# A channel gate streamed through SBUF: three slots of 84 rows in place of four of 60, with smaller first tiles and gates in two parts

## The chip, the cores and the metric

The kernel runs on one core of one Trainium2 chip. The metric is device time in microseconds, the median of several runs. A run has one launch, with its inputs and its output in HBM. Beside the times there is one profiled execution, whose trace all views below are read from; its span runs from the first to the last instruction.

## The reference

The input `x` has 384 x 384 pixels of 384 channels in bf16, `w1d` is a single number. Each channel is averaged over all pixels, the average is multiplied by `w1d` and put through a sigmoid, and every pixel of the channel is multiplied by the result:

```python
g = jnp.einsum("bhwc->bc", x) / (H * W)
gp = jnp.pad(g, ((0, 0), (pad, pad)))          # k = 1, pad = 0
s = jnp.zeros_like(g)
for i in range(k):
    s = s + gp[:, i:i + C] * w1d[i]
s = _sigmoid(s)
return x * s[:, None, None, :]
```

The input and the output have 113.25 MB each. Taken literally, the input has to be read twice, since the mean needs all of it before the first product.

## The kernel before

**Tiling.** The pixels are spread over 128 partitions. One "row" in what follows is one pixel of 384 channels on each partition (768 B per partition), so there are 1,152 rows. A large SBUF buffer, `arena`, holds four slots of `TILE` = 60 rows and, behind them at `base`, the `FIRST` = 12 rows. The rest of the input makes 19 tiles of 60 rows, and tile k lives in slot k mod 4.

**The early gate.** The kernel guesses the gate: it sums only the first `EARLY` = 4 rows (`sum_first`, three matmuls with a matrix of ones), makes the sigmoid of that (`s_early`), and multiplies every tile by it as the tile comes in (`gate`, L204 to 207, a multiplication in place on VectorE). Meanwhile it also sums all of `x`: TensorE adds the first 52 rows of each tile (`sum_others`, 39 matmuls per tile into three PSUM banks), and VectorE the last `OWN` = 8 (`sum_own`, a reduction, L327, and an addition, L334). At the end the two sums are joined (`join_own`, `add_banks`), the true gate `s_true` is made (L474) and compared with `s_early` (L482 to 496). The flag `redo` says whether they differ in bf16. Only then would a second pass read everything again (`again`); it isn't run on these inputs.

**Order.** A small planner class (`Planner`) writes one list of instructions per engine in program order. For each instruction it derives the waits from the rows that it reads and writes. SP issues all loads but three halves, ACT issues all stores; an engine's list is strictly in order, so a wait holds up all that is behind it. Loads of the first four tiles are issued at once, three of them as two halves of 30 rows on SP and on ACT (`BOTH` = 3). One DMA of each queue is put ahead of the barrier at the kernel's start (`ahead`). From tile 4 on, a load waits for the store that empties its slot.

**The pause.** Ahead of the first such load stands `pause` (L387): a dummy activation on ACT that starts when store 0 has landed. ACT's list there is store 0, store 1, the pause, store 2.

**TensorE's loop.** The sums of the tiles are one hardware loop; each turn waits for one count of the semaphore `ready`, which GpSimd raises when a tile has landed (`relay`). Ahead of the loop TensorE waits for all `FIRST` rows (`plan.need`, L446). VectorE's gate of a tile has to wait for TensorE's sum of the same tile, because it overwrites the rows.

**The end.** The last tile is gated into another slot, so that its gate needn't wait for its sum. Then come its own reduction, the gate and the store of the 12 first rows, and the check. SP, ACT and VectorE read the flag, and ACT waits for all stores.

Of the kernel before, what the change touches and what calls it, by code (L numbers as in the profile page):

```python
# [3 lines left out]
P = 128  # L4
ROW = 384
BF16 = mybir.dt.bfloat16
# [3 lines left out]
ACT_F = mybir.ActivationFunctionType  # L10
# [139 lines left out]
def split(n, most):  # L150
    k = -(-n // most)
    return [n // k + (i < n % k) for i in range(k)]


WIDE = 512

FIRST, EARLY, TILE, SLOTS, BOTH, OWN, PAUSE = 12, 4, 60, 4, 3, 8, 8  # L160


def bass_standalone__channel_attn_eca__vision_kernel(
# [5 lines left out]
    B, H, W, C = x.shape  # L169
    assert B == 1 and C == ROW and (B * H * W) % (4 * P) == 0  # L170
    n_rows = B * H * W // P
    x_rows, o_rows = x.flatten_outer_dims(), out.flatten_outer_dims()

    def dram(view, r0, n):
        return view[r0 * P : (r0 + n) * P, :].rearrange("(p t) c -> p (t c)", p=P)

    ones = nc.alloc_sbuf_tensor("ones", [P, P], BF16)
    s_early = nc.alloc_sbuf_tensor("s_early", [P, C], BF16)
    w_one = nc.alloc_sbuf_tensor("w_one", [1, 16], BF16)
    w_scaled = nc.alloc_sbuf_tensor("w_scaled", [P, 2], F32)  # L180
    warm = nc.alloc_sbuf_tensor("warm", [P, 2], F32)
    wrong = nc.alloc_sbuf_tensor("wrong", [P, 1], F32)
    redo = nc.alloc_sbuf_tensor("redo", [P, 1], I32)
    total = nc.alloc_sbuf_tensor("total", [P, C], F32)
    own = nc.alloc_sbuf_tensor("own", [P, C], F32)
    part = nc.alloc_sbuf_tensor("part", [P, C], F32)
    terms = nc.alloc_sbuf_tensor("terms", [P, 3 * C], BF16)
    n_arena = nc.sbuf_bytes_remaining // (2 * C)
# [8 lines left out]
    def at(r0, n):  # L197
        assert r0 + n <= n_arena
        return arena[:, r0 * C : (r0 + n) * C]

    def rows(r0, n):
        return [("sb", r) for r in range(r0, r0 + n)]

    def gate(to, place, n, s):  # L204
        s_b = s[:].unsqueeze(1).broadcast_to([P, n, C])
        v, to_v = (at(r, n).rearrange("p (t c) -> p t c", t=n) for r in (place, to))
        return lambda e: e.tensor_tensor(to_v, v, s_b, ALU.mult)  # L207

    n_tiles = (n_rows - FIRST) // TILE
    base = SLOTS * TILE  # L210
    assert (n_rows - FIRST) % TILE == 0 and base + FIRST + 1 + PAUSE <= n_arena
    assert FIRST % 4 == EARLY % 4 == (TILE - OWN) % 4 == 0 and EARLY + 4 < FIRST
    last = n_tiles - 1
    ready = nc.alloc_semaphore("ready")

    def slot(k):
        return k % SLOTS * TILE

    def row0(k):
        return FIRST + k * TILE  # L220


    s_true = at(base + FIRST, 1)
    plan = Planner(nc, "a", 70)

    def load(place, n, r0, queues=("sync",), reads=()):
        i = 0
        for queue, m in zip(queues, split(n, -(-n // len(queues)))):
            plan.dma(
                queue,  # L230
                at(place + i, m),
                dram(x_rows, r0, n)[:, i * C : (i + m) * C],
                reads=reads,
                writes=rows(place + i, m),
            )
            i += m
# [19 lines left out]
    def add_rows(e, group, column, n, start, stop):  # L256

        n_wide = n * C // WIDE
        all_of = [
            mm(  # L260
                e,
                acc[group][i % 3][:, :],
                ones[:],
                arena[:, column + i * WIDE : column + (i + 1) * WIDE],
                start and i < 3,
                stop and i >= n_wide - 3,
            )
            for i in range(n_wide)
        ]
        return all_of[-1]  # L270
# [8 lines left out]

    def sum_others():  # L280

        def one(e, s):
            e.wait_ge(ready, 1).then_inc(ready, -1)  # L283
            add_rows(e, 1, slot(s) * C, TILE - OWN, False, False).then_inc(
                plan.sems["tensor"], 1
            )

        def emit(e):
            add_rows(e, 1, (base + EARLY) * C, 4, True, False)
            rounds = -(-n_tiles // SLOTS)  # L290
            some = n_tiles - (rounds - 1) * SLOTS
            with e.Fori(0, rounds) as k:
                for s in range(some):
                    one(e, s)
                if some < SLOTS:
                    with e.If(k < rounds - 1):
                        for s in range(some, SLOTS):
                            one(e, s)
            add_rows(
                e, 1, (base + EARLY + 4) * C, FIRST - EARLY - 4, False, True  # L300
            ).then_inc(plan.sems["tensor"], 1)

        plan.streams["tensor"].append(("block", emit, None))

# [15 lines left out]
    def sum_own(k):  # L320

        r0 = slot(k) + TILE - OWN
        view = at(r0, OWN).rearrange("p (t c) -> p c t", t=OWN)
        to = part if k else own
        plan.op(
            "vector",
            lambda e: e.reduce_sum(to[:], view, axis=mybir.AxisListType.X),  # L327
            reads=rows(r0, OWN),
            writes=["part" if k else "own"],
        )  # L330
        if k:
            plan.op(
                "vector",
                lambda e: e.tensor_tensor(own[:], own[:], part[:], ALU.add),  # L334
                reads=["own", "part"],
                writes=["own"],
            )
# [34 lines left out]
            writes=["total"],  # L372
        )

    def put(place, n, r0, to=None):
        to = place if to is None else to
        plan.op(
            "vector",
            gate(to, place, n, s_early),
            reads=["s_early"] + rows(place, n),  # L380
            writes=rows(to, n),
        )
        plan.final.append(
            plan.dma("scalar", dram(o_rows, r0, n), at(to, n), reads=rows(to, n))
        )

    def pause(r0):  # L387

        to = at(base + FIRST + 1, PAUSE)
        plan.op(  # L390
            "scalar",
            lambda e: e.activation(  # L392
                to, warm[:, 0:1].broadcast_to([P, PAUSE * C]), ACT_F.Sigmoid
            ),
            reads=["warm"],
            writes=rows(r0, 1) + ["pause"],
        )

    def weight():

# [23 lines left out]

    plan.op("gpsimd", lambda e: e.memset(warm[:, 0:1], 0.0), writes=["warm"])
    plan.op("vector", lambda e: e.memset(ones[:], 1.0), writes=["ones"])  # L426
    load(base, FIRST, 0)
    for k in range(BOTH):
        load(slot(k), TILE, row0(k), ("sync", "scalar"))
        if k == 0:  # L430
            plan.dma("scalar", w_one[0:1, 0:1], w1d.unsqueeze(0), writes=["w_one"])
    for k in range(BOTH, SLOTS):
        load(slot(k), TILE, row0(k))
    heads = {e: len(plan.streams[e]) for e in ("sync", "scalar")}
    weight()
    sum_first()
# [6 lines left out]
        reads=["total", "w_scaled0", "warm1"],  # L443
        writes=["s_early"],
    )
    plan.need("tensor", rows(base, FIRST))  # L446
    sum_others()

    for k in range(n_tiles):
        if k >= SLOTS:  # L450

            for i in range(2) if k == SLOTS else () if k < SLOTS + 2 else (k - SLOTS,):
                sum_own(i)
                put(slot(i), TILE, row0(i))
            if k == SLOTS:
                pause(slot(k))
            load(slot(k), TILE, row0(k), reads=["pause"] if k == SLOTS else ())
        there = rows(slot(k), TILE)
        plan.relay(ready, "gpsimd", "tensor", there, there, ["acc1"])
    plan.signals("tensor", rows(base, FIRST), ["acc1"])  # L460
    for k in range(n_tiles - SLOTS, last):
        sum_own(k)
        put(slot(k), TILE, row0(k))

    put(slot(last), TILE, row0(last), slot(n_tiles))
    sum_own(last)
    put(base, FIRST, 0)
    join_own()


# [30 lines left out]


    again = Planner(nc, "b", 30)
    half, r0 = base // 2, 0
    for k, n in enumerate(split(n_rows, half)):
        place = k % 2 * half
        again.dma("sync", at(place, n), dram(x_rows, r0, n), writes=rows(place, n))
        again.op(
            "vector",
            gate(place, place, n, s_true),  # L510
            reads=rows(place, n),
            writes=rows(place, n),
        )
        again.final.append(
            again.dma("scalar", dram(o_rows, r0, n), at(place, n), reads=rows(place, n))
        )
        r0 += n
# [4 lines left out]
    def ahead(name, e, n):  # L522

        block = nc.main_func.blocks[0].instructions
        at_end = len(block)
        plan.emit(name, e, n)
        new = block[at_end:]  # L530
        del block[at_end:]
        barrier = next(
            i
            for i, ins in enumerate(block)
            if ins.engine == e.engine and isinstance(ins, mybir.InstDrain)
        )
        block[barrier:barrier] = new

    ahead("sync", nc.sync, 1)
    ahead("scalar", nc.scalar, 1)  # L540
    plan.emit("sync", nc.sync, heads["sync"] - 1)
    plan.emit("scalar", nc.scalar, heads["scalar"] - 1)

    with nc.Block() as block:
# [66 lines left out]
```

## Time and profile before

| | us |
|---|---|
| median of 3 runs (lowest, highest) | 528.31 (528.24, 528.57) |
| the profiled execution | 528.49 |
| its span | 527.0 |
| TensorE matmuls busy | 198.5 |
| VectorE busy | 353.9 |
| ScalarE busy | 5.5 |
| mean DMA rate over the span | 430 GB/s |
| a store of 60 rows (5,760 KB), issue to landing, median | 47.4 |
| a load of 60 rows, issue to landing, median | 38.9 |

In the page's view of slices, each of the 40 columns is 13.2 us; the row "DMA" gives the busy share of the 16 DMA engines in tenths and the row below it what they moved. A line of the timeline reads: start, duration, engine, source line, operation, what is written and read, shape, and in brackets how long the engine stood idle before it and what ended that. A line with "SPq" or "ACTq" is the issue of a DMA by that engine's queue, not the transfer; where several are merged, the duration runs from the first to the last. In the view of waits the columns are the total, the number of waits and the longest.

### The profile page before, as it was taken

The page shows a single profiled execution, that of the slowest core. Times are in us where ns is not written, and L with a number is a line of the kernel's source. Part 1 is how long each engine was busy: PE and PEld are TensorE (multiplying, and loading weights), DVE is VectorE, ACT ScalarE, POOL GpSimd, SP SyncE. Part 2 cuts the span into 40 slices and gives each one's busy share as a digit, 9 for nine tenths or more (in the row PEclk, how much of TensorE's full clock was granted, in tenths as well). Part 3 has the DMA queues.
Part 4 walks back from the last instruction along what each step waited for, and adds up shares of the span by engine and source line. Part 5 has one row for each costly group of instructions (what it writes and reads, how often), then busy time and mean ns, then how long its engine had stood idle before and what let it go on. Part 6 is the DMA issues. An engine that isn't in the chain of part 4 may idle for free. (4 is left out here: it accounts for less than half of the span.)

```text
span 527.0 us, 1015 instructions
## 1 busy us (share of the span) xinstructions
PE 198.5 (38%) x754; PEld 0.2 (0%) x2; DVE 353.9 (67%) x81; ACT 5.5 (1%) x5; POOL 0.3 (0%) x5
## 2 busy tenths in 40 slices
PE   0389170070706151524333342516060707070810
PEld 0000000000000000000000000000000000000000
DVE  0639999649494858576666666666666666758892
ACT  1000020000000000000000000000000000000000
POOL 0000000000000000000000000000000000000000
PEclk9999766576767667675758585858585858585765
DMA  9999999999999999999999999999999999999998
GB/s 383 434 421 418 448 448 395 444 448 448 395 444 448 448 395 444 448 444 399 444 448 444 399 444 448 445 399 444 444 444 406 441 444 444 406 441 444 444 406 363
DMA packets 6196, 226.51 MB, mean 430 GB/s; under 512 B 690, under 2 KB 690, under 8 KB 690
## 3 DMA queue, kind: packets, MB, share of 16 engines
q10 hardware_dynamic: 3314, 122.10, 53.6%
q1 hardware_dynamic: 2880, 104.40, 46.1%
q14 instruction: 2, 0.02, 0.0%
HBM read 113.25 MB, written 113.25 MB: 430 GB/s over the span
## 5 line engine op out<-in xcount | busy, mean ns | idle before, releaser
L244 PE MATMUL acc<-arena,ones 128*128 128x512 bf16 x749 | 196.6, 429 | 288.4 <-PEq L283 288.4
L207 DVE TENSOR_TENSOR arena<-arena,s_early 128x23040 bf16<-128x23040 bf16 (+1 forms) x20 | 233.5, 11677 | 78.0 <-PE acc L244 73.6
L327 DVE TENSOR_REDUCE part<-arena 128x384 f32<-128x3072 bf16 x18 | 96.4, 5355 | 67.3 <-DMA arena<-in_x_dram 67.3
L334 DVE TENSOR_TENSOR own<-own,part 128x384 f32<-128x384 f32 x18 | 10.0, 558 | 0.6
L418 DVE TENSOR_SCALAR w_scaled<-w_all 128x1 f32<-128x1 f32 x2 | 0.2, 152 | 14.3 <-PE w_all L409 14.3
L409 PE MATMUL w_all<-w_one,ones 1*128 1x1 bf16 x1 | 0.2, 158 | 15.3 <-DMA w_one<-in_w1d_dram 15.3
L244 PE MATMUL acc_own<-terms,ones 128*128 128x384 bf16 x3 | 1.4, 479 | 10.5 <-DVE terms L345 10.5
L327 DVE TENSOR_REDUCE own<-arena 128x384 f32<-128x3072 bf16 x1 | 5.3, 5305 | 0.0
L474 ACT ACTIVATE arena<-total,w_scaled 128x384 bf16<-128x384 f32 x1 | 0.6, 615 | 439.0 <-DVE total L315 439.0
L315 DVE TENSOR_TENSOR total<-total,acc 128x128 f32<-128x128 f32 (+2 forms) x11 | 4.5, 408 | 0.4
L392 ACT ACTIVATE arena<-warm 128x3072 bf16<-128x3072 f32 x1 | 2.8, 2763 | 54.1 <-DMA out_dram<-arena 54.1
L313 DVE COPY total<-acc 128x384 f32<-128x384 f32 x1 | 0.6, 558 | 1.2 <-PE acc L244 1.2
L403 ACT ACT_TABLE_LOAD x1 | 1.3, 1283 | 2.3 <-issue 2.3
L352 DVE TENSOR_TENSOR own<-own,terms 128x384 f32<-128x384 f32 x2 | 1.1, 558 | 0.1
L345 DVE CAST terms<-own 128x384 bf16<-128x384 f32 x3 | 1.1, 357 | 0.1
L482 DVE TENSOR_TENSOR total<-arena,s_early 128x384 f32<-128x384 uint16 x1 | 0.6, 557 | 0.7 <-ACT arena L474 0.7
L370 DVE TENSOR_TENSOR total<-total,acc_own 128x384 f32<-128x384 f32 x1 | 0.6, 554 | 0.6 <-PE acc_own L244 0.6
L426 DVE MEMSET ones<- 128x128 bf16 x1 | 0.2, 165 | 1.0 <-PEq L596 1.0
L440 ACT ACTIVATE s_early<-total,w_scaled 128x384 bf16<-128x384 f32 x1 | 0.6, 615 | 15.8 <-DVE total L315 15.8
L242 PE MATMUL acc<-arena,ones 128*128 128x512 bf16 x1 | 0.6, 608 | 0.0
L490 DVE TENSOR_REDUCE wrong<-total 128x1 f32<-128x384 f32 x1 | 0.6, 552 | 0.0
L403 ACT ACTIVATE warm<-warm 128x1 f32<-128x1 f32 x1 | 0.2, 203 | 0.0
(8 smaller groups left out, 0.9 us busy)
## 6 DMA issues: line engine op xcount, KB each, us to landing
out_dram<-arena ACTq DMA_DIRECT2D x19, 5760.0 KB, 47.4
arena<-in_x_dram SPq DMA_DIRECT2D x16, 5760.0 KB, 38.9
arena<-in_x_dram ACTq DMA_DIRECT2D x3, 2880.0 KB, 27.4
arena<-in_x_dram SPq DMA_DIRECT2D x3, 2880.0 KB, 36.4
arena<-in_x_dram SPq DMA_DIRECT2D x1, 1152.0 KB, 10.3
out_dram<-arena ACTq DMA_DIRECT2D x1, 1152.0 KB, 16.9
w_one<-in_w1d_dram ACTq DMA_DIRECT2D x1, 0.0 KB
```

What stands on the lines that cost most here:

```text
L207: return lambda e: e.tensor_tensor(to_v, v, s_b, ALU.mult)
L242: loaded.append(e.matmul(bank, weights, moving, start=start, stop=stop))
L244: return e.add_instruction(mybir.InstMatmult(name=nc.get_next_instruction_name(), engine=mybir.EngineType.PE, ins=[e.lower_ap(moving), e.l ...
L313: emit = lambda e, part=part, of=of: e.tensor_copy(part, of)
L315: emit = lambda e, part=part, of=of: e.tensor_tensor(part, part, of, ALU.add)
L327: lambda e: e.reduce_sum(to[:], view, axis=mybir.AxisListType.X),
L334: lambda e: e.tensor_tensor(own[:], own[:], part[:], ALU.add),
L345: lambda e, term=term: e.tensor_copy(term, own[:]),
L352: lambda e, term=term: e.tensor_tensor(own[:], own[:], term, ALU.subtract),
L370: lambda e: e.tensor_tensor(total[:], total[:], acc_own[:, :C], ALU.add),
L392: lambda e: e.activation(to, warm[:, 0:1].broadcast_to([P, PAUSE * C]), ACT_F.Sigmoid),
L403: lambda e: e.activation(warm[:, 1:2], warm[:, 0:1], ACT_F.Sigmoid),
```

## The change

- Three slots of 84 rows (`SLOTS`, `TILE`) stand in place of four of 60. The first rows are 8 in place of 12, tile 0 has 52 rows (`HEAD`), and 13 tiles of 84 rows follow it.
- TensorE sums 72 rows of a tile in two parts, 44 (`HALF`) and 28, with a signal after each; VectorE's own share is 12 rows. Tile 0 has no such share: TensorE sums its 52 rows, and 20 rows behind them that GpSimd has set to zero.
- The gate of a tile is two instructions, rows 0 to 44 as soon as the first part is summed, and the rest after the second. The own rows are reduced ahead of both. Each tile is still stored in one DMA, but the last, whose two parts are stored separately.
- The first 8 rows are gated and stored right after tile 0, not at the end. TensorE closes its sums with three matmuls of zeros.
- Loads at the start: rows 0 to 4 on SP, then `w1d` (on ACT before), then tile 0 as two halves of 26 rows, then rows 4 to 8 as two loads of two rows, one on each queue, then tile 1 as two halves of 42, then tile 2. Two DMAs of SP stand ahead of the barrier.
- The pause is five activations of 1,344 elements in place of one of 3,072.

```diff
-FIRST, EARLY, TILE, SLOTS, BOTH, OWN, PAUSE = 12, 4, 60, 4, 3, 8, 8
+FIRST, EARLY, HEAD, TILE, SLOTS, BOTH = 8, 4, 52, 84, 3, 2
+HALF, OWN = 44, 12
+PAUSE, PAUSES = 1344, 5
...
         def one(e, s):
             e.wait_ge(ready, 1).then_inc(ready, -1)
-            add_rows(e, 1, slot(s) * C, TILE - OWN, False, False).then_inc(
-                plan.sems["tensor"], 1
-            )
+            for r, n in ((0, HALF), (HALF, TILE - OWN - HALF)):
+                add_rows(e, 1, (slot(s) + r) * C, n, False, False).then_inc(done, 1)
 
         def emit(e):
-            add_rows(e, 1, (base + EARLY) * C, 4, True, False)
+            add_rows(e, 1, (base + EARLY) * C, 4, True, False).then_inc(done, 1)
...
-            add_rows(
-                e, 1, (base + EARLY + 4) * C, FIRST - EARLY - 4, False, True
-            ).then_inc(plan.sems["tensor"], 1)
+            for i in range(3):
+                out = mm(e, acc[1][i][:, :], ones[:], none, False, True)
+            out.then_inc(done, 1)
...
+    def put(k):
+        if k:
+            sum_own(k)
+        gated(slot(k), 0, HALF)
+        gated(slot(k), HALF, size(k))
+        store(slot(k), size(k), row0(k), 0, size(k))
+
+    def put_last():
+
+        for lo, hi in ((0, HALF), (HALF, TILE)):
+            gated(slot(last), lo, hi, slot(n_tiles))
+            store(slot(n_tiles), TILE, row0(last), lo, hi)
+        sum_own(last)
+
+    def put_first():
+        gated(base, 0, FIRST)
+        store(base, FIRST, 0, 0, FIRST)
...
-        to = at(base + FIRST + 1, PAUSE)
-        plan.op(
-            "scalar",
-            lambda e: e.activation(
-                to, warm[:, 0:1].broadcast_to([P, PAUSE * C]), ACT_F.Sigmoid
-            ),
-            reads=["warm"],
-            writes=rows(r0, 1) + ["pause"],
-        )
+        to = at(base + FIRST + 1, 4)[:, :PAUSE]
+        of = warm[:, 0:1].broadcast_to([P, PAUSE])
+        for i in range(PAUSES):
+            plan.op(
+                "scalar",
+                lambda e: e.activation(to, of, ACT_F.Sigmoid),
+                reads=["warm"],
+                writes=["pause"] + ([] if i else rows(r0, 1)),
+            )
...
-    load(base, FIRST, 0)
-    for k in range(BOTH):
-        load(slot(k), TILE, row0(k), ("sync", "scalar"))
+    pad = rows(slot(0) + HEAD, TILE - OWN - HEAD)
+    plan.op("gpsimd", lambda e: e.memset(zeros[:], 0.0), writes=["zeros"])
+    plan.op(
+        "gpsimd", lambda e: e.memset(at(slot(0) + HEAD, len(pad)), 0.0), writes=pad
+    )
+    load(base, FIRST, 0, hi=EARLY)
+    plan.dma("sync", w_one[0:1, 0:1], w1d.unsqueeze(0), writes=["w_one"])
+    for k in range(SLOTS):
+        both = ("sync", "scalar") if k < BOTH else ("sync",)
+        load(slot(k), size(k), row0(k), both)
         if k == 0:
-            plan.dma("scalar", w_one[0:1, 0:1], w1d.unsqueeze(0), writes=["w_one"])
-    for k in range(BOTH, SLOTS):
-        load(slot(k), TILE, row0(k))
+            load(base, FIRST, 0, both, lo=EARLY)
...
-    plan.need("tensor", rows(base, FIRST))
+    plan.need("tensor", ["zeros"] + rows(base, FIRST))
     sum_others()
+    plan.signals("tensor", rows(base, FIRST), ["acc1"])
 
     for k in range(n_tiles):
+        if k == SLOTS:
+            put(0)
+            put_first()
+            put(1)
+            pause(slot(0))
+        elif k > SLOTS + 1:
+            put(k - SLOTS)
         if k >= SLOTS:
...
             load(slot(k), TILE, row0(k), reads=["pause"] if k == SLOTS else ())
```

## The prediction

> **What bounds the kernel now.** I read the page's slices and queues first, then the waits of SP's own queue, then the timeline at both ends.
>
> ```profile
> DMA  9999999999999999999999999999999999999998
> GB/s 383 434 421 418 448 448 395 444 448 448 395 444 448 448 395 444 448 444 399 444 448 444 399 444 448 445 399 444 444 444 406 441 444 444 406 441 444 444 406 363
> ...
> q10 hardware_dynamic: 3314, 122.10, 53.6%
> q1 hardware_dynamic: 2880, 104.40, 46.1%
> ```
>
> The two rings (q1 is SP's, q10 is ACT's) fill 53.6 + 46.1 = 99.7% of the span on 16 engines. The dips to 395 are no gaps: a slice of 13.2 us holds seven or eight turns of the 16 engines. So the kernel is bound by moving 226.5 MB. The trace's records of single packets (one packet is one partition's row of a transfer) have medians of 347, 855 and 1702 ns for 9,216, 23,040 and 46,080 B: 36.76 ns per 1,000 B and 8 ns per packet. One tile row (768 B on each of 8 partitions of an engine) costs 0.226 us. All 2,304 rows, in and out, cost 520.3 us, and 43 transfers of 8 packets per engine add 43 x 8 x 8 ns = 2.8: 523.1 of the 527.0 us. Only the other 4 us and the 2.8 can be won; what can be lost is any time in which both rings are empty.
>
> ```profile
> SPq L109 <- DMA out_dram<-arena: 368.8, 14, 26.9
> SPq L109 <- ACT arena L392: 74.2, 1, 74.2
> ```
>
> A load waits only for the store that empties its slot; the first such load waits for the pause on ACT as well.
>
> ```profile
> 24.18 11.17 PE L244 MATMUL acc<-arena,ones 128*128 128x512 bf16 x39 [6.04 <-PEq L283]
> 35.45 12.16 DVE L207 TENSOR_TENSOR arena<-arena,s_early 128x23040 bf16<-128x23040 bf16 x1 [10.63 <-PE acc L244]
> ...
> 47.64 18.36 ACTq L109 DMA_DIRECT2D out_dram<-arena  x2
> ...
> 53.47 12.15 DVE L207 TENSOR_TENSOR arena<-arena,s_early 128x23040 bf16<-128x23040 bf16 x1
> ...
> 74.31 2.76 ACT L392 ACTIVATE arena<-warm 128x3072 bf16<-128x3072 f32 x1 [54.06 <-DMA out_dram<-arena]
> ```
>
> This is the one place where the cover is thin. The four slots hold 252 rows of loads (57 us); the first store goes out at 47.6, the second at 65.7 (47.64 + 18.36 less an issue of 0.35), and the fifth load, behind the pause, at 77.1. By the packet records SP's ring is empty from 67.1 to 80.5, and store 0 and store 1 carry that stretch alone.
>
> ```profile
> 489.55 12.16 DVE L207 TENSOR_TENSOR arena<-arena,s_early 128x23040 bf16<-128x23040 bf16 x1 [4.38 <-DMA arena<-in_x_dram]
> ...
> 501.63 5.29 DVE L327 TENSOR_REDUCE part<-arena 128x384 f32<-128x3072 bf16 x1
> ...
> 507.43 2.55 DVE L207 TENSOR_TENSOR arena<-arena,s_early 128x4608 bf16<-128x4608 bf16 x1
> ...
> 517.94 0.15 DVE L496 CAST redo<-wrong 128x1 int32<-128x1 f32 x1
> ```
>
> The last load lands at 489.5, the check is ready at 518.1, and the last store lands at 526.9: the check has 9 us to spare.
>
> **What the Trainium skill says.** "DMA: Bandwidth & Descriptors", section "Queues, rings and completion order": an engine takes turns between its rings packet by packet. The trace agrees, 347 ns packets of SP alternating one to one with 855 ns packets of ACT in its first 10 us; so a transfer of tiny rows beside one of long rows goes at the pace of the long ones. Same page, "Where 436 GB/s comes from": a ceiling of 435.2 GB/s; the slope above, 36.76 ps per byte on each of 16 engines, gives 435. "VectorE: DVE Perf Modes", section "The TRN2 errata": a fixed cost per instruction. Here: 12.158 us for 23,040 and 2.551 for 4,608 elements give 0.521 ns per element and 0.149 us fixed. "TensorE: Matmul & The Clock Gate", "What's actually happening": half clock until some 3.4 us of work. Here, in windows of 2 us, 5, 7 and 7 matmuls run in the first 5.8 us from 24.18, then 11 per window.
>
> **The change part by part**, against this execution.
>
> Fewer, longer packets. After: 19 loads and 16 stores, 35 transfers for 43, all bytes the same. 8 x 8 x 8 ns = -0.5 us (by the mean in place of the median, -0.7). A row of 84 has 64,512 B, 2.38 us a packet; no trace shows that size. I take the same slope, since 9 to 46 kB lie on one line.
>
> Start. SP's first transfer shrinks from 12 rows to 4. ACT's first packet comes at 2.7, SP's at 1.0; in between SP moved about 4 packets of 9 kB per engine and now at most 8 of 3 kB: 12 kB less, +0.45 us (0 to 0.6). w1d moves to SP, one issue (0.50 in the old place) ahead of the barrier: all queues start 0.5 later, hidden behind packets in flight. It lands early, no longer at 15.2; s_early comes at about 12, needed only at 30. ACT loses that issue. The GpSimd memset of 7,680 elements is unseen in the trace. "GPSIMD Engine Reference", "Elementwise", has 1.03 to 2.6 cycles per element at 1.2 GHz: an estimate of 6.6 to 16.6 us from 1.5, so done by 8 to 18; I take 10, hidden behind the loads.
>
> First store. By the packet records the engines lag 1.8 us behind their summed work in the first 50 us, and 2.7 from the first store on; with the 0.45 from above 2.25 and 3.15. Rows 0 to 58 take 13.1 us of engine time, so tile 0 is moved at 15.4 and landed at about 16.5. But rows 4 to 8, two on each queue, come behind tile 0's halves, and PE must have them first (the need ahead of the loop). ACT's half started earlier and ends earlier; its 2 rows slip between SP's long packets, and SP's 2 rows then meet the 42-row packets of tile 1, 1.20 us each. Bounds: none of the 8 turns (landed 16.7) or all (26); I take 4: 20.5. PE then does 3 + 33 matmuls, 11.17 less three of 0.18 = 10.6: 31.1. DVE: 44 rows (16,896 elements) 8.95, 8 rows 1.75 (PE's other 21 matmuls end meanwhile, at about 35), store 0 at 42; rows 0 to 8 1.75; the 12-row reduction of tile 1, unseen: in proportion to 5.36 it is 8.04; at one element per 0.96 GHz cycle with the rest fixed, 6.96; I take 8.0; then 8.95 + 8.15. Together 37.55, and store 1 goes out at 69 (65 to 74).
>
> What is left to move by then: 228 rows of loads and the 60 of store 0 and the first rows, 288 x 0.226 and 0.8 for 13 transfers = 65.9, with the lag of 3.15: the rings run dry at 69.0. Store 1's first packet needs 1.0 (SP at the start) to 2.6 (ACT at the start) after its issue; with 1.5, 70.5. Nothing else can fill in: load 3 sits behind the pause, and the pause on ACT's queue behind store 1. So a gap of +1.5 us (0 to 4).
>
> Pause. Five activations of 1,344 elements for one of 3,072: 2,763 against 615 ns for 384 elements gives 1.38 each, 6.9 in all. Load 3 goes out at 76. Store 1 alone lasts 19 us: 0.
>
> Steady state. Period 168 x 0.226 + 0.13 = 38.1. DVE 8.0 + 0.56 + 8.95 + 8.15 = 25.7 of it; PE 54 x 0.264 = 14.3. Splitting the gate costs 0.15 and starts it after 33 matmuls: hidden, 0. A slot's round: load 36 + landing 2.7, DVE 25.7, store 36 + 2.7, and two first packets of 4.8 to 7.7 (3.4 and 5.5 in the trace, longer by 84/60): 113 to 119 against 3 x 38.1 = 114.3. A ring may thus run dry, but the other then has the full rate; both are dry only if one transfer ends within the start of the next. I take 0; 1 us a period would be +11.
>
> End. Last load to flag: 8.95 + 8.15 + 8.0 + 0.56 + 8.2 (509.89 to 518.09) = 33.9, SP's reading 1.65: 35.6. Stores left at that landing: tile 13's 84 rows and most of tile 12's, 32 to 37 us. The spare 9 us are gone; 0 taken, up to +2. The halved last store keeps the ring fed: the first half is ready 9 us after the landing, under tile 12's store.
>
> Sum: -0.5 + 0.45 + 1.5 = +1.45, span 528.45. This execution took 528.49, 1.5 around its span and 0.2 over the median 528.31; on the median: **529.8 us**.
>
> **Rivals.** *No gap.* The small rows land with tile 0, or the reduction is the cheap one. For: their packets are 64 ns. Against: turns are one to one. -0.5 + 0.45 = -0.05: 528.3, no change. *Faster.* The tail decides: the engines end unevenly, 1.1 us of engine time is idle in the last 2 us (240 GB/s from 524 to 526), the start 1.3. If there is no gap, the packets bring 0.7, the start loses nothing and half the tail loss goes, -1.25: 527.1. It decides only if the gap is under 0.2 us. *Three slots or the end.* Both rings dry in the loop, or the flag after the stores: +3 to +11, 534. For: a round trip at its limit and no spare at the end. Against: two of three slots are always in transfer.
>
> **How the numbers follow.** About 0.2% (1.06 us) can be told from no change. Gap, 529.8 (528.7 to 532.3): 0.58, of it 0.08 within 0.2%. No gap 0.24. Faster 0.08. Slots or end 0.10. Slower 0.50 + 0.10 = 0.60, same 0.24 + 0.08 = 0.32, faster 0.08. The range 527.7 to 532.3 leaves out the last two cases.
>
> **What would show it.** Right: a slice of low GB/s at 66 to 71 us, none later; the first PE block beginning after 18 us; store 1 issued after 67; 2.38 us packets. Wrong: PE starting at 17 and no low slice; low slices once a period; the flag after 525.

## The result, and the profile after

| | before | after |
|---|---|---|
| median (lowest, highest), us | 528.29 (528.24, 528.57) | 546.75 (543.17, 550.41), 4 runs |
| the profiled execution, us | 528.49 | 550.41 |
| its span, us | 527.0 | 548.9 |
| last load lands, us | 489.5 | 513.0 |
| check ready, us | 518.1 | 546.6 |

The changed kernel takes 1.0349 of the time before, with a 95% interval of 1.028 to 1.0418. The profiled execution is the longest of the four; all sums below are made on the two profiled executions, whose spans differ by 21.9 us. Medians here and below are of all runs of a kernel, while ratios and intervals leave out runs over 1.5% above its fastest.

The page of the changed kernel, its slices of 13.7 us and its queues:

```profile
DMA  9999999999999999999899999999999999999895
GB/s 384 436 437 394 412 432 395 428 432 418 451 423 423 404 428 442 437 418 437 329 409 432 404 395 451 385 442 452 376 423 418 437 447 395 409 414 447 385 405 215
...
q10 hardware_dynamic: 2736, 120.13, 51.5%
q1 hardware_dynamic: 2306, 106.37, 46.2%
```

Before, the two rings (SP's and ACT's queues) filled 99.7% of the span, now 97.7%, and that understates the loss: a packet that takes longer than its bytes need also counts as busy. Over half the slices were at 440 to 448 GB/s before; now few are, with 329 in one (261 to 274 us) and 215 in the last.

The waits of SP's queue, after:

```profile
SPq L109 <- DMA out_dram<-arena: 384.7, 10, 53.9
...
SPq L109 <- ACT arena L433: 72.4, 1, 72.4
```

SP waits for ten stores, 38 us each and 54 in one case; before it was 14 of at most 27. That alone is no loss: with fewer and larger tiles there are fewer and longer waits. Whether the rings had anything left meanwhile decides.

The start, in the timeline of the changed kernel:

```profile
20.98 26.49 PE L254 MATMUL acc<-arena,ones 128*128 128x512 bf16 x109 [13.87 <-DMA arena<-in_x_dram]
31.39 12.30 DVE L212 TENSOR_TENSOR arena<-arena,s_early 128x16896 bf16<-128x16896 bf16 x3 [21.55 <-PE acc L254]
42.05 26.77 ACTq L109 DMA_DIRECT2D out_dram<-arena  x3
...
68.87 6.74 ACT L433 ACTIVATE arena<-warm 128x1344 bf16<-128x1344 f32 x5 [58.38 <-DVE arena L212]
```

TensorE begins at 20.98 (20.5 was forecast), store 0 goes out at 42.05 (42), store 1 at 68.49 (42.05 + 26.77 less an issue of 0.33; 69 was forecast). By the packet records the 16 engines stand idle for 1.2 us in the mean between 68.1 and 69.4, all at once for 0.9 us. That is the forecast gap.

Windows of 20 us in the loop, after; the columns are busy time of PE, PEld, DVE, ACT and POOL with their counts, then the granted clock, the DMA share and GB/s:

```profile
240.00:260.00 20.00, 11.20 (x49) 0.00 (x0) 19.73 (x4) 0.00 (x0) 0.00 (x0) 0.84 1.00 435
260.00:280.00 20.00, 3.89 (x10) 0.00 (x0) 7.80 (x2) 0.00 (x0) 0.00 (x0) 0.50 0.86 332
280.00:300.00 20.00, 10.67 (x45) 0.00 (x0) 18.25 (x4) 0.00 (x0) 0.00 (x0) 0.84 1.02 442
300.00:320.00 20.00, 3.57 (x10) 0.00 (x0) 6.95 (x2) 0.00 (x0) 0.00 (x0) 0.52 0.99 387
```

The second window is the low slice. In the fourth the engines count as 99% busy but move only 387 GB/s: its packets take longer than their bytes need. The timeline around the second window shows what the rings wait for:

```profile
237.95 7.98 DVE L339 TENSOR_REDUCE part<-arena 128x384 f32<-128x4608 bf16 x1 [18.64 <-DMA arena<-in_x_dram]
...
246.75 17.03 DVE L212 TENSOR_TENSOR arena<-arena,s_early 128x16896 bf16<-128x16896 bf16 x2 [0.23 <-PE acc L254]
263.81 0.34 ACTq L109 DMA_DIRECT2D out_dram<-arena  x1
266.46 0.33 SPq L109 DMA_DIRECT2D arena<-in_x_dram  x1
275.98 7.94 DVE L339 TENSOR_REDUCE part<-arena 128x384 f32<-128x4608 bf16 x1 [12.20 <-DMA arena<-in_x_dram]
```

A tile lands at 237.95 and is on its way out only at 263.81, 25.9 us later. ACT's ring got nothing new until then. Most engines had by then finished the store before it and SP's current load as well: at 263 only three of the 16 have a packet. These three go on with the load to 273.2, and it counts as landed only at 276, with the slowest. The next load waits for a store until 266.46.

The end, after:

```profile
513.01 17.03 DVE L212 TENSOR_TENSOR arena<-arena,s_early 128x16896 bf16<-128x16896 bf16 x2 [13.86 <-DMA arena<-in_x_dram]
...
522.00 8.41 ACTq L109 DMA_DIRECT2D out_dram<-arena  x2
...
529.96 7.85 DVE L339 TENSOR_REDUCE part<-arena 128x384 f32<-128x4608 bf16 x1
...
546.48 0.15 DVE L540 CAST redo<-wrong 128x1 int32<-128x1 f32 x1
```

The last load lands 23.5 us later than before. From there the flag takes 33.6 us, and the last store lands at 546.3, 0.3 us before the flag is written.

**Where the 21.9 us went.** From the packet records I take, for each stretch, the time in which the 16 engines had no packet (idle) and the time that packets took beyond 36.76 ns per 1,000 B and 8 ns each (longer), both as a mean over the engines, in us (some packet records overlap, so each column of figures comes to 0.8 or 0.9 more than its span):

| stretch | before: idle, longer | after: idle, longer | difference |
|---|---|---|---|
| 0 to 60 | 1.34, 1.56 | 1.20, 1.57 | -0.1 |
| 60 to 120 | 0.01, 0.01 | 1.17, 2.07 | +3.2 |
| 120 to 46 before the last DMA's end | 0.09, 0.13 | 3.21, 9.86 | +12.9 |
| the last 46 | 1.13, 0.03 | 4.79, 0.33 | +4.0 |
| last DMA to the end of the span | 0.54 | 2.98 | +2.4 |
| the bytes and packets themselves | 523.1 | 522.6 | -0.5 |

The sum is +21.9. Most of it lies where the prediction put 0.

### The profile page after: what moved, and what is told of

Read it like the earlier page. It is cut to its first block, busy times and chain, and to the rows that moved or that the text cites. A ratio compares the mean times of both kernels' runs of the same rounds, so it can differ in the third digit from the quotient of the medians.

```text
span 548.9 us, 996 instructions
## 1 busy us (share of the span) xinstructions
PE 193.7 (35%) x755; PEld 0.2 (0%) x2; DVE 352.9 (64%) x78; ACT 9.3 (2%) x9; POOL 6.8 (1%) x7
## 5 line engine op out<-in xcount | busy, mean ns | idle before, releaser
L254 PE MATMUL acc<-arena,ones 128*128 128x512 bf16 x747 | 191.1, 420 | 329.8 <-PEq L296 315.2
L212 DVE TENSOR_TENSOR arena<-arena,s_early 128x16896 bf16<-128x16896 bf16 (+2 forms) x29 | 233.6, 8100 | 42.0 <-PE acc L254 28.2
L339 DVE TENSOR_REDUCE part<-arena 128x384 f32<-128x4608 bf16 x12 | 95.6, 7965 | 142.7 <-DMA arena<-in_x_dram 142.7
L339 DVE TENSOR_REDUCE own<-arena 128x384 f32<-128x4608 bf16 x1 | 7.9, 7918 | 0.0
L433 ACT ACTIVATE arena<-warm 128x1344 bf16<-128x1344 f32 x5 | 6.6, 1323 | 58.5 <-DVE arena L212 58.4
L346 DVE TENSOR_TENSOR own<-own,part 128x384 f32<-128x384 f32 x12 | 6.7, 558 | 0.4
L469 POOL MEMSET arena<- 128x7680 bf16 x1 | 6.5, 6498 | 0.0
L252 PE MATMUL acc<-arena,ones 128*128 128x512 bf16 x1 | 0.6, 607 | 0.0
```

Of the source, the lines that this page charges most:

```text
L252: loaded.append(e.matmul(bank, weights, moving, start=start, stop=stop))
L254: return e.add_instruction(mybir.InstMatmult(name=nc.get_next_instruction_name(), engine=mybir.EngineType.PE, ins=[e.lower_ap(moving), e.l ...
L433: lambda e: e.activation(to, of, ACT_F.Sigmoid),
L469: "gpsimd", lambda e: e.memset(at(slot(0) + HEAD, len(pad)), 0.0), writes=pad
```

## The experiments

Theory S: with three slots of 84 rows the trip of a slot (in, gated, out, free again) is as long as three periods, so both rings run dry in the loop. Rival G: the new order of the work costs it (own rows reduced ahead of the gates, gates in two parts, first rows behind tile 0). Rival P: it is the packets of 64.5 kB. The loss column below is idle and longer together in the loop (from 120 us to 46 us before the last DMA's end); "last 16" is the time over which the last 16 packets of a transfer end, as a mean over the loop's loads and stores, in us.

| kernel | median us | ratio to before | slots | load packet, kB | loop's loss | last 16: loads, stores |
|---|---|---|---|---|---|---|
| before | 528.29 | | 4 | 46.1 | 0.2 | 2.1, 2.4 |
| after | 546.75 | 1.0349 | 3 | 64.5 | 13.1 | 9.6, 8.2 |
| four slots | 532.27 | 1.0055 | 4 | 46.8 | 1.6 | 5.3, 4.7 |
| before with three | 549.15 | 1.0405 | 3 | 46.1 | 9.4 | 2.3, 1.7 |
| no own rows | 544.21 | 1.0267 | 3 | 64.5 | 9.3 | 8.3, 12.1 |
| short packets, first attempt | 534.98 | 1.0114 | 3 | 32.3 | 0.3 | 2.2, 1.1 |
| short trip | 538.44 | 1.0197 | 3 | 64.5 | 2.2 | 6.7, 3.8 |
| packets only | 532.85 | 1.0087 | 3 | 32.3 | 0.3 | 0.9, 0.9 |
| halves | 528.98 | 1.0010 | 3 | 33.8 and 30.7 | 0.4 | 0.7, 0.7 |
| early half | 529.27 | 1.0019 | 3 | 64.5 | 1.1 | 1.8, 2.9 |
| rows first | 546.42 | 1.0329 | 3 | 64.5 | 10.6 | 9.5, 10.3 |
| packets, rows first | 534.51 | 1.0110 | 3 | 32.3 | 0.3 | 1.9, 1.4 |
| long trip | 533.59 | 1.0103 | 3 | 32.3 | 0.8 | 0.8, 0.8 |
| longer trip | 544.91 | 1.0293 | 3 | 32.3 | 11.2 | 1.7, 1.6 |

The packet records don't name the engine, so the last column is a guess at how far the engines are apart. Other records bear it out: a transfer's semaphore rises in 16 counts as it lands, and from the first to the last count it takes 2.1 us for loads and 2.6 for stores before, 9.7 and 8.5 after, 0.9 and 0.9 in packets only (means over the same stretch). In four slots the column is too low: the counts there are 8.1 and 14.1 us apart.

**Four slots.** The changed kernel, with its order, in four slots of 61 rows:

```diff
-FIRST, EARLY, HEAD, TILE, SLOTS, BOTH = 8, 4, 52, 84, 3, 2
-HALF, OWN = 44, 12
+FIRST, EARLY, HEAD, TILE, SLOTS, BOTH = 8, 4, 46, 61, 4, 2
+HALF, OWN = 32, 9
```

> The changed kernel with four slots of 61 rows in place of three of 84 (tile 0 of 46 rows, own share 9, gate parts of 32 and 29); everything else of the change stays. Theory S, three slots leave no reserve: a slot's round trip (two transfers, landings, VectorE, two first packets, some 113 to 119 us) is as long as three periods of 38.1, so both rings run dry; with four slots of 61 there are four periods of 27.7 = 110.7 for a trip of about 85, and the time goes back to 527 to 530. Theory G, the new order (gates in two parts, own rows ahead of them, first rows early) is what costs: it stays at 540 or more.

532.27 us (528.51 to 539.47, 20 runs), interval of the ratio 1.0029 to 1.0081. The loop's loss falls from 13.1 to 1.6: the order of the work doesn't make it. The profiled execution is the longest but one of the 20 (539.1 us). In it 15 engines land the last store between 525.2 and 528.7, and one at 537.6. The counts of its loads and stores are apart all through the loop, with packets of 46.8 kB, and yet the loop loses only 1.6: as long as the slots leave room, engines that are apart cost it little. Why one engine lags, and why these runs spread so far, I didn't settle. This run changes the slots and the packet's length together.

**Before with three.** The kernel before, with one slot less and the rest as it was:

```diff
-FIRST, EARLY, TILE, SLOTS, BOTH, OWN, PAUSE = 12, 4, 60, 4, 3, 8, 8
+FIRST, EARLY, TILE, SLOTS, BOTH, OWN, PAUSE = 12, 4, 60, 3, 3, 8, 8
```

> The kernel before with three slots of 60 rows in place of four, nothing else. Theory S: three periods of 27.2 = 81.6 us for a round trip of 85 to 90 (load 26 + 2, VectorE with TensorE 22.8, store 26 + 2, two first packets of 3.4 to 5.5): both rings run dry, each tile takes 1 to 3 us longer, 18 tiles: 548 to 580. Theory G, the order of the change costs and not the slots: 528 to 531.

549.15 us, interval 1.034 to 1.047. The slices of this kernel:

```profile
DMA  9998699999999999999999999999999999999978
GB/s 382 431 431 350 293 404 431 434 431 431 431 428 431 431 428 374 434 434 431 431 431 380 431 431 431 431 432 374 431 431 431 431 431 367 431 431 434 431 333 356
```

Three slots lose 9.4 us in the loop with the old order and 46 kB packets too: a dip to 367 to 380 about every 82 us, the time in which three tiles of 60 rows go in and out (3 x 27.3). The gap at the start is large here (slices of 350 and 293), since three slots of 60 rows cover less of it: 8.7 us idle before 120, where the kernel before has 1.4.

**No own rows.** From tile 2 on, the 12 rows of VectorE are left out of the sum that the check compares:

```diff
-        if k:
+        if k == 1:
             sum_own(k)
```

> The changed kernel without the reductions of the own rows from tile 2 to tile 12 and their additions (left out: the share of those rows in the sum for the check, which then has a wrong sum but still agrees in its flag or runs a second pass; the gates and the stores are the same). VectorE's part of a slot's round trip falls by 8.5 us, from 25.7 to 17.1. Theory S says that the round trip is what counts, whatever it is made of: 8.5 us less in 114 gives the reserve back, and the time falls to 528 to 534 (if no second pass runs; with one it is near twice as long). If the loss is in the transfers themselves (packets of 64.5 kB slow beside each other), it stays within 3 us of 546.

544.21 us, interval 1.0225 to 1.0309: little won. The trace tells why this run says nothing on the trip: the first gate still waits for 33 matmuls, which now run where the reduction ran, and a load that landed at 313.5 is stored from 339.7 on, 26.2 us later, about as in the changed kernel (25.9 above).

**Short trip.** This takes away what that run left. TensorE sums only 4 rows of each part, and VectorE's share is left out from tile 2 on, so that all other rows are missing from the check's sum; the trip gets some 7.5 us shorter, and packets and slots stay:

```diff
-                add_rows(e, 1, (slot(s) + r) * C, n, False, False).then_inc(done, 1)
+                add_rows(e, 1, (slot(s) + r) * C, 4, False, False).then_inc(done, 1)
...
-        if k:
+        if k == 1:
             sum_own(k)
```

> The changed kernel in which TensorE sums only 4 rows of each part of a tile and VectorE reduces no own rows from tile 2 to tile 12 (left out: most of the sum for the check; gates, loads and stores are the same, in packets of 64.5 kB). From a load's landing to its store's issue it needs 1.3 us of matmuls and 17.1 of gates in place of 26: a round trip 7.5 us shorter. In the run without the reductions alone, TensorE's 33 matmuls took the place of the reduction and the trip stayed as long (26 us by its trace), so it told nothing of the trip's length. Theory S (the length of the trip against three periods decides, whatever it is made of): the rings hardly run dry, 528 to 534. Theory P (long packets cost by themselves): within 4 us of the changed kernel's 546.75.

Its timeline for one tile:

```profile
251.43 38.52 ACTq L109 DMA_DIRECT2D out_dram<-arena  x2
...
271.07 2.72 PE L254 MATMUL acc<-arena,ones 128*128 128x512 bf16 x6 [35.47 <-PEq L296]
272.55 17.03 DVE L212 TENSOR_TENSOR arena<-arena,s_early 128x16896 bf16<-128x16896 bf16 x2 [21.16 <-PE acc L254]
```

The load that landed at 270.9 is stored from 289.6 on (251.43 + 38.52 less an issue of 0.34), 18.7 us later.

538.44 us, interval 1.0161 to 1.0233. The loop's loss falls from 13.1 to 2.2 and the last load lands at 501.3 instead of 513.0; the gap at 66 to 69 is gone as well. The rest stays: the last 46 us idle for 4.9, as in the changed kernel (4.8), and the span ends 5.8 us after the last DMA (3.0 there). So S holds for the loop, and the end has a loss of its own.

**Short packets, first attempt.** Loads and stores in two DMAs of 42 rows each; a load waits for the whole slot:

```diff
-        store(slot(k), size(k), row0(k), 0, size(k))
+        m = size(k) // 2
+        store(slot(k), size(k), row0(k), 0, m)
+        store(slot(k), size(k), row0(k), m, size(k))
...
```

> The changed kernel with each load (from tile 3 on) and each store made as two DMAs of 42 rows issued one behind the other, so that packets have 32 kB in place of 64.5; a load still waits for the whole tile's store. Theory P, the long packets cost: the wait for a first packet (4.4 to 6.4 us after the issue of a load) and the landing (2.7 us after the last packet) are two and one packets of the other ring, and halve; a round trip gets 5 to 7 us shorter, and the time falls to 530 to 538. Theory S, the number of slots alone: those 5 us are part of the trip too, but if most of the loss is the uneven end of the 16 engines it stays at 541 to 549.

534.98 us, interval 1.0056 to 1.0172, with runs from 532.13 to 544.56 and no loss in the loop. It proves little: its first half of a store goes out after the first gate part, 8 us earlier, so that the trip is shorter too.

**Packets only.** The same, but both halves of a store wait for both gate parts, as the whole store did:

```diff
+        plan.need("scalar", rows(slot(k), size(k)))
         store(slot(k), size(k), row0(k), 0, m)
         store(slot(k), size(k), row0(k), m, size(k))
```

> The changed kernel with loads and stores as two DMAs of 42 rows each, and now both halves of a store wait for both parts of the gate (in the first run with short packets the first half went out after the first part, 8 us early, so the trip was shorter for two reasons). Only the packets differ: 32 kB in place of 64.5. Theory P: as in that run, 530 to 536. Theory S: the trip gets shorter by half of two first-packet waits and of two landings, some 5 to 7 us, and the time falls by part of the loss, to 532 to 541. If it stays over 543, packets are no part of it.

532.85 us (532.61 to 533.62), interval 1.007 to 1.0103. The same three slots, the same order, the same work on VectorE, a store that leaves 26.8 us after its tile's landing (26.3 in the changed kernel, both means over the loop), and the loop loses 0.3. The run has twice the transfers along with half the packet, and doesn't tell these two apart. Its slices:

```profile
DMA  9998999999999999999999999999999999999997
GB/s 386 447 466 359 427 397 423 394 437 440 430 435 432 430 430 435 440 432 432 435 428 430 435 437 435 432 435 428 430 440 430 435 435 435 428 432 440 428 436 325
```

From slice 8 on the rate hardly moves. What is left against before is the gap (1.15 idle and 1.8 longer between 60 and 120), twice the packets' fixed cost (524.1 us of bytes and packets against 523.1), and the check, ready 2.2 us after the last DMA (DMA alone would be done at 528.9 of 531.1).

**Halves.** The store of a half goes out right after its gate part, and the load of a half waits for its own half; nothing is left out:

```diff
-        gated(slot(k), 0, HALF)
-        gated(slot(k), HALF, size(k))
-        store(slot(k), size(k), row0(k), 0, size(k))
+        for lo, hi in ((0, HALF), (HALF, size(k))):
+            gated(slot(k), lo, hi)
+            store(slot(k), size(k), row0(k), lo, hi)
...
-            load(slot(k), TILE, row0(k), reads=["pause"] if k == SLOTS else ())
+            for lo, hi in ((0, HALF), (HALF, TILE)):
+                load(slot(k), TILE, row0(k), lo=lo, hi=hi, reads=["pause"] if k == SLOTS else ())
```

> The changed kernel in which each tile is stored in two DMAs, each right after its part of the gate, and the next load of the slot is two DMAs of 44 and 40 rows, each waiting for its own half of the store. Nothing is left out. Theory S: a half's round trip is shorter by about 8 us of VectorE and half a transfer, some 25 us, so the rings never run dry in the loop; what remains is the end, where the last landing to the flag takes 35.6 us: 527.5 to 532. If stragglers among the 16 engines are the cause by themselves, it stays over 535.

528.98 us (median of 20), interval 1.0003 to 1.0017: the best with three slots, and not faster than before. Its timeline at the start shows where the gap went:

```profile
39.64 28.46 ACTq L109 DMA_DIRECT2D out_dram<-arena  x5
```

The first half of store 0 goes out 2.4 us earlier and the first of store 1 some 8 us ahead of its second; the stretch from 60 to 120 has 0.03 us idle.

**Early half.** Only the stores are in halves, the loads stay whole, with packets of 64.5 kB (the first part of the diff above).

> The changed kernel in which only the stores are split, each half right after its part of the gate; loads stay whole, in packets of 64.5 kB, and wait for both halves. The trip is shorter by 8 us of VectorE and by about 4 us of first packet and landing of the store. Theory S: 528 to 535. Theory P, if long loads cost: 538 or more.

529.27 us, interval 1.0006 to 1.0033. So loads with 64.5 kB packets are not slow in themselves. In 27% of the loop's engine time ACT's ring alone has packets, since SP's runs dry in every tile; yet no engine idles, and the loop loses 1.1. One dry ring costs next to nothing as long as the other has packets.

**Rows first.** To close the gap, all 8 first rows are loaded in one DMA ahead of tile 0, so that TensorE need not wait for four of them behind tile 0:

```diff
-    load(base, FIRST, 0, hi=EARLY)
+    load(base, FIRST, 0)
...
-        if k == 0:
-            load(base, FIRST, 0, both, lo=EARLY)
```

> The changed kernel with its first 8 rows loaded in one DMA ahead of tile 0, in place of 4 rows ahead and 2 + 2 behind it; nothing else. TensorE then waits for tile 0 alone and begins at about 17 in place of 21, and store 1 goes out at 64.5 in place of 68.5, before the rings run dry at 68 to 69. The gap of the prediction's first-store step goes: about 3 us of the changed kernel's loss (1.2 of idle engines and 2.1 of longer packets when the loads start again at 79). Theory S says that the loop loses as much as before: 541 to 546. If the loss of the loop were a late consequence of that gap (a phase set at the start), it would fall under 536.

> The run that differs from the changed kernel in its packets alone (532.85), with the first 8 rows loaded in one DMA ahead of tile 0. Its loop loses nothing, so what the gap at 68 us costs is seen alone: 1.15 of idle engines and 1.8 of longer packets, 3 us less: 529.5 to 530.5. If longer packets at the restart have another cause than the dry rings, only the 1.15 go: 531.5.

Both fell short: 546.42 us (1.026 to 1.0397) on the changed kernel, and 534.51 (1.0092 to 1.0128) with the short packets, 1.66 more than without the edit. The timeline of the second:

```profile
23.15 26.13 PE L254 MATMUL acc<-arena,ones 128*128 128x512 bf16 x106 [12.00 <-PEq L296]
...
43.87 27.26 ACTq L109 DMA_DIRECT2D out_dram<-arena  x5
```

The rows now delay SP's half of tile 0, which lands at 23.0; TensorE begins 2.2 us later than in the changed kernel and store 1 goes out at 70.3. The miss still gives a measurement: the idle time of the gap grew from 1.15 to 3.12 us and the kernel by 1.66, so idle time there costs nearly one for one. The longer packets behind the gap stayed at 1.8 us. They don't grow with the idle time before them.

**Long trip.** The kernel of packets only, with the own rows reduced a second time from tile 2 on, 8 us more of VectorE. The store then leaves 33.5 us after the landing in place of 26.8, 6.7 later; the rest of the 8 falls into VectorE's waits for TensorE:

```diff
+        if k > 1:
+            r0 = slot(k) + TILE - OWN
+            view = at(r0, OWN).rearrange("p (t c) -> p c t", t=OWN)
+            plan.op(
+                "vector",
+                lambda e: e.reduce_sum(part[:], view, axis=mybir.AxisListType.X),
+                reads=rows(r0, OWN),
+                writes=["part"],
+            )
```

> The run that differs from the changed kernel in its packets alone (32 kB; 532.85, no loss in the loop), with the own rows of tiles 2 to 12 reduced twice (the same result written again), 8 us more of VectorE in each slot's round trip; VectorE is then at 34 of 38.1 us. Theory S: the trip gets longer by as much as the short packets had saved and a little more, the rings run dry in the loop again: 536 to 548. Theory P, the length of a packet by itself: unchanged within 1 us, 532 to 534.

533.59 us, interval 1.0074 to 1.0133: the loop loses 0.8. S with the numbers that I had given it was wrong here; either the packets alone decide, or the short ones leave more than 6.7 us of room.

**Longer trip.** The same kernel, with nine activations on ACT ahead of each store from tile 2 on, in place of the reduction:

```diff
+    late = at(base + FIRST + 1, 4)[:, :PAUSE]
...
+        if k > 1:
+            for i in range(9):
+                plan.op(
+                    "scalar",
+                    lambda e: e.activation(late, warm[:, 0:1].broadcast_to([P, PAUSE]), ACT_F.Sigmoid),
+                    reads=["warm"],
+                    writes=["pause"],
+                )
```

> The kernel of the short packets and late first half store (532.9 us), with nine activations of 1,344 elements on ScalarE ahead of each tile's stores from tile 2 on: 9 x 1.32 = 11.9 us more on a slot's trip, with nothing more on VectorE and nothing left out. The long-trip run added its 8 us on VectorE and lost only 0.8 us in the loop. Theory S, in which a trip longer than three periods dries both rings: the trip is now well beyond three periods, the engines idle in every tile, the loop loses 5 us or more, 537 to 550 us. Theory P, in which the length of a packet decides: 532 to 536 us, the loop's loss stays under 1 us. If it loses, the longer packets after the idle time are to be seen again at about 2 us per event, also with rows of half the length.

544.91 us, interval 1.0261 to 1.0325. Its group of activations, its slices, and the timeline of one tile:

```profile
L421 ACT ACTIVATE arena<-warm 128x1344 bf16<-128x1344 f32 x99 | 130.9, 1322 | 300.0 <-DVE arena L212 297.2
```

```profile
DMA  9999899999999999999999999999998999997998
GB/s 380 430 454 449 361 403 430 411 421 445 388 411 421 445 416 421 438 433 428 371 445 426 402 423 419 447 421 433 374 440 388 416 414 416 454 416 305 416 427 368
```

```profile
275.33 17.03 DVE L212 TENSOR_TENSOR arena<-arena,s_early 128x16896 bf16<-128x16896 bf16 x2 [1.00 <-PE acc L254]
292.39 12.15 ACT L421 ACTIVATE arena<-warm 128x1344 bf16<-128x1344 f32 x9 [22.77 <-DVE arena L212]
298.79 8.00 DVE L339 TENSOR_REDUCE part<-arena 128x384 f32<-128x4608 bf16 x1 [6.43 <-DMA arena<-in_x_dram]
...
303.22 0.82 ACTq L109 DMA_DIRECT2D out_dram<-arena  x2
```

The gate ends at 292.4 and the store leaves at 303.2, as the last of the nine activations starts. Over the loop it leaves 37.6 us after the landing in the mean, 10.8 later than in packets only. The dips are back, with packets of 32 kB: the loop is idle for 2.7 us and its packets are longer by 8.5, 11.2 together against 0.3 without the activations; the total rises by 12.06. So P alone doesn't make the loss. What fits both runs is that packet length acts through the room that it leaves: at 32 kB that lies between 6.7 and 10.8 us, if it is all one where on the trip they are spent (VectorE in the run before, ACT here); at 64.5 kB there is none, since the changed kernel needs a shorter trip to get rid of its loss.

## Why the prediction was wrong

**Right: the packets, the start, the gap.** The packet of 64,512 B has a median of 2,380 ns against 2.38 us taken; the reduction of 12 rows 7.97 us against 8.0; the memset on GpSimd 6.5 us, just under the lower end of the estimate (6.6), and hidden. The three times of the start hit within 0.5 us, and the gap came at its place. Part of that is luck: TensorE's 20.5 was picked between bounds of 16.7 and 26, and the gap's size, +1.5 forecast and 1.2 measured, comes of two misses that partly cancel (the rings were dry at 68.4, not 69.0, and the first packet of store 1 came 0.84 us after its issue, not 1.5). But behind it, at 79 to 82, when SP's ring starts again beside ACT's, packets take 2.07 us longer in sum. The step had no term for that, and the gap cost 3.2.

**Wrong: "Steady state", where it says "I take 0".** The step had nearly the right sum: a slot's round of 113 to 119 us against 114.3. It let the sum pass because "both are dry only if one transfer ends within the start of the next". Measured from landing to landing in the same slot, a round takes 117 to 127 us, 119.8 in the mean. Two terms of the sum were off, in opposite directions: a load takes 40.8 us and a store 39.3 from first to last packet, where 36 each was taken, and the two first packets come to 7.8 in place of 9.6 to 15.4. The runs show +12.9 us where the step had 0 (its price for the other case, 1 us a period or +11, was close), and three things that it left out:

- *There was no room, and the step counted none.* In the kernel before, the first packet of a load comes 10.6 to 11.3 us after the load's issue, and that of a store 18.4 to 19.3 us after its own: behind each issue stands work that its ring has yet to finish. In the changed kernel it is 3.5 to 7.6 for the nine loads issued between 110 and 470 us, and for four of nine stores 0.85, the value of an engine with nothing to do. A ring that starts anew loses next to nothing by itself (the early half shows it); here both do so within 10 us (ACT's at 264.7, SP's at 272.5).
- *The 16 engines are not one.* In the changed kernel they are level up to 148 us (the last 16 packets of that load end within 1.5 us), and from the load that ends at 191 on these packets end over 8.6 to 11.7 us. A transfer lands with its slowest engine, so this is added to the trip, while the fast engines idle. Before it was 2.1 us, and with short packets 0.9. The sum of the step had a landing time of 2.7 us, which is also what a landing takes behind the last packet (2.72), but nothing for engines out of step.
- *A restart costs more than the time that was idle.* Of the loop's 13.1 us only 3.2 are idle, and 9.9 are longer packets, most of them (7.0) at four places: 1.7 to 1.8 us for each engine near 272, 310, 391 and 470. These lie behind just the four stores whose first packet came 0.85 us after the issue, where SP's next load starts 6 to 8 us later; behind the two stores between them it is 0.4 and 0.2. Idle engines alone don't tell these places: at the lowest point 13, 1, 12 and 12 of the 16 had no packet, never all. In the kernel before with three slots the same shows behind four loads (first packet after 0.94 to 0.97 us, then 1.3 to 2.0 us longer).

What is shown: a slot less makes the loss in the kernel before; a fourth slot, a shorter trip, or shorter packets take nearly all of it away from the changed kernel, whose order stays as it is; and with short packets 10.8 us more of trip bring it back, where 6.7 don't. That the packet's length works through the room on the trip is argued from these runs. What stays open: why packets are longer after a restart, and what puts the engines out of step. The length of the packet alone doesn't (the early half has 64.5 kB loads and 1.8 us; in four slots they are out of step at 46.8 kB), and neither does dry time alone (the longer trip has 11.2 us of loss and 1.7).

**Wrong: "End", "0 taken, up to +2".** The duration was right: 35.6 us from the landing to the flag read, measured 35.9 to the end of the span. The stores didn't fill it: at that landing the rings had 28.1 us of work left, where 32 to 37 was taken. The 16 counts of the last load come over 11.2 us (1.0 in packets only, with 33.6 us of work left), so while the slowest engine was still loading, others did stores that were to fill the end. The engines are then idle for 4.8 us in the last 46, against 1.1 before; and the flag is read 2.4 us later behind the last DMA than before: 4.0 + 2.4 = +6.4 in all. The short trip keeps this loss (4.9 idle) with nearly none in the loop, so it belongs to the end. In packets only the idle part goes (0.5) and the late check stays, 2.2 us behind the last DMA; in the halves both are gone.

**The rivals.** "Three slots or the end" was the case that came, at +18.5 on the medians where it was given +3 to +11: it took both rings being dry as the whole price, and neither the longer packets nor two losses at once. Of the signs of being wrong, the flag after 525 came (546.6), and low slices in the loop, though not once a period. "No gap" and "faster" fell with the gap.

## What to carry to other kernels

With fewer slots than before, work out a slot's whole trip against the period times the slots, and when it comes out even, as here, count it as a loss and not as zero: transfers land with the slowest engine, and a restart costs more than its idle time. The time between a transfer's issue and its first packet helps to see how much room there is. In this case 10 to 19 us went with room and 0.85 to 1 us with the loss; 3.4 to 5 us stood on both sides (packets only, the changed kernel) and tells nothing. If large tiles are wanted for few instructions, let each part of a tile be stored and loaded on its own: with that three slots of 84 rows came within 0.2% of four slots of 60.

## What was not expected of the hardware

- When a ring starts on engines with nothing to do and the second ring starts beside it 6 to 12 us later, each engine's packets take 1 to 2 us longer in sum: behind the gap at the start 1.8 at 32 kB (after 1.15 and 3.12 us of idle time alike) and 2.07 at 64.5 kB, in the loop 1.7 to 1.8 in the changed kernel and 1.05 to 1.46 in the longer trip. Not all 16 engines need be idle for it.
- From the last packet of a transfer to its landing, with the other ring active, it takes 2.05 to 2.18 us at 46 kB, 2.7 at 64.5 kB and mostly 1.5 to 1.7 at 32 kB; with the other ring empty, 0.3 to 0.6.
- A ring that starts on idle engines has its first packet 0.85 us after the issue (ACT's) or 0.94 to 1.04 (SP's); beside an active ring with 64.5 kB packets it takes 3.5 to 6.1.
